# Last output weights read twice in small pieces, operands of the cosine layers moved in time

## The chip, the cores and the metric

One core of a Trainium2 chip runs the whole program in one launch. The time is that of the device, in microseconds, from runs of the same program on the same kind of chip; the kernel before has a median of 1354.78 us in three runs (1353.57 to 1355.01).

## What is computed

Three parts follow each other. Attention with a window of 128 and 4 sink positions gives 1536 rows of 512. Eight experts, weighted by a matrix that is normalised by rows and columns in turn, work on these rows; then two dense layers with a cosine between them.

```python
x = attention(q, k, v)                       # 1536 x 512
P = sinkhorn(exp(x @ w_gate - max))          # 1536 x 8, eight rounds
out = sum over e of P[:, e:e+1] * (relu(x @ w1[e]) @ w2[e])      # w1[e]: 512 x 1024, w2[e]: 1024 x 512
h = out @ w_in                               # 512 x 2048
result = (h * cos(h)) @ w_out                # 2048 x 512
```

## The kernel before

**Layers, batches, stages.** The 1536 rows are two batches of 768. Ten layers run one after the other: e = 0 to 7 are the experts, e = 8 and 9 the two halves of the dense block, each with 1024 of the 2048 hidden columns. Each layer runs on batch 0 and then on batch 1. One layer on one batch is called a stage here and written (e, b), so the cosine stages are (8,0), (8,1), (9,0) and (9,1), in this order.

**A stage.** The first product uses a scheme with seven products in place of eight. Every 32-bit operand is split into a 16-bit high half and a low half, and a product takes three matmuls per pair (high by high, high by low, low by high). In a cosine stage `g1_sums` makes, for each of four column groups j, the seven products in the order o = 0, 4, 1, 5, 2, 3, 6; each is six matmuls into one of five PSUM banks (`ring["g1"]`). The product o = 0 is copied out by ScalarE (L1007), the others are taken up by VectorE adds (L999). `act_cos` then makes h cos(h) for each of four sums per j: ScalarE L893, VectorE L896, ScalarE L901 and L902, VectorE L905, and GpSimd L907 and L909, which write the two halves of `hh`. The second product (`g2_mm`, L1036) takes `hh` and `W2S[e % 2]`, the split w2; part of it is done between the products of `g1_sums` from j = 1 on, in the order f = 0, 4, 1, 5, 2, 6, 3, 7 of the eight pieces of hidden columns.

**Ticks.** The order of all work outside these loops is written by hand. `tick()` is called after each product of the first kind and after each two f of the second: 28 ticks (`GT`) in the first part of a stage, 24 (`HT_`) in the second, 104 in a layer. `put(t0, every, steps)` puts steps at a tick, counted from the call. A tick only says where in each engine's queue an instruction stands; an engine goes through its queue as fast as its operands allow. `late` holds what is put into the queues one tick after.

**Splitting.** `split` (L190, L191) has ScalarE write the high half (a scaled copy) and, one tick later, VectorE the low half from the source and the high half. The scale comes from `scales`: a row maximum, some short VectorE operations, one small TensorE product with a diagonal matrix (L142, L149) to bring the maximum over the partitions together, and four short VectorE operations.

**Weights of layer e + 1** are made ready while layer e runs. `w_load` reads the tensor in four pieces of 512 KB into the one buffer `st`; a maximum of each piece follows, then the scale, then the split. For the first product (`w1_split`) GpSimd makes four sums `S` for each j (L274 to L277) into one of the two buffers with the tag `f64`, and ScalarE and VectorE split them into `W1O`; there is only one `W1O`, so this runs while the second part of (e, 1) runs. For w2 of layer 9 the maximum of a piece is a maximum of squares on ScalarE (L171, `junk` takes the unused output). Its reads stand at tick 0 of layer 8, the squares at ticks 6, 11, 16 and 21, the scale at 26, the eight splits from tick 41 on, every 1.4 ticks. The reads of w1 follow into the same `st` at tick 51, the maxima at 57 to 66, its split at ticks 90 to 97. `w2_first` is used for layer 0 alone: it reads w2 in four pieces into `f64` buffers, once for the maxima and once more for the split.

**Operands of layer 8.** `x2(b)` is called once the experts are summed in `ACC`. For each batch it makes six operands by `x_operand`: three sums on GpSimd (L205 to L207), three splits into a tile `xs` with the tag `f64`, and, after four ticks, a DMA that transposes `xs` into `XO[b]` (L213, issued by SP). All products of a stage read all six. Batch 0's six stand at ticks 5, 12, 19, 26, 33 and 40 of (7,1), batch 1's at ticks 5, 12, 19, 37, 41 and 45 of (8,0). SP's queue also issues the weight reads (L242 in `w_load`, L1123 in `w2_first`) and the output writes.

Of the kernel before, what the change touches and what calls it, by code (L numbers as in the profile page):

```python
# [12 lines left out]
BF16 = mybir.dt.bfloat16  # L13
# [27 lines left out]
def kernel(  # L41
# [14 lines left out]
    nc = tc.nc  # L56
# [746 lines left out]
    def experts(before):  # L803
# [60 lines left out]
        def x2(b):  # L864

            a = ACC[b]
            m = sm.tile([128, NT], F32, tag="x2m", name="x2m")

            def scl():
                m1 = sm.tile([128, 1], F32, tag="x2n", name="x2n")  # L870
                nc.vector.tensor_reduce(out=m1, in_=m, axis=AX.X, op=ALU.max)
                scales(m1, 1, 1e-30, res, f"x2{b}", lambda *s: sx2.__setitem__(b, s))

            def ops(c, i):
                put(2, 1, [x_operand(b, c, i, sx2[b][0])])
# [166 lines left out]
        def layers(e, b, act, so):  # L1042
# [24 lines left out]
            if e == E - 1:  # L1067
                amx, xops = x2(b)

                put(5, 4, [amx[t] for t in tiles])  # L1070
                put(26, 1, amx[-1:])
                if b:

                    put(HT_ + 5, 7.0, xops[:3])
                    put(HT_ + GT + 9, 4.0, xops[3:])
                else:
                    put(HT_ + 5, 7.0, xops)
            late = None
# [35 lines left out]

        def w2_first():

            m = sm.tile([128, NJ], F32, tag="wm", name="wm")
            src = w_src(0, "w2")
            box = {}

            def load(n):
                t = box[n] = stage.tile([128, 2, 512], F32, tag="f64", name="w2p", bufs=2)
                nc.sync.dma_start(out=t, in_=src[:, 2 * (n % NJ):2 * (n % NJ) + 2, :])  # L1123

            def amax(n):
                absmax(m[:, n:n + 1], box.pop(n).rearrange("p a b -> p (a b)"))

            def scl():
                m1 = sm.tile([128, 1], F32, tag="wmm", name="wmm")
                nc.vector.tensor_reduce(out=m1, in_=m, axis=AX.X, op=ALU.max)  # L1130
                scales(m1, 1, 1e-30, res, "w20", lambda *s: wsc.update({(0, "w2"): s}))

            def sp(n):
                f = slice(2 * (n % NJ), 2 * (n % NJ) + 2)
                split(W2S[0][:, 0, f], W2S[0][:, 1, f], box.pop(n), wsc[0, "w2"][0])

            for n in range(2 * NJ):
                put(3.5 * n, 1, [lambda n=n: load(n)])
                put(3.5 * n + 3, 1, [lambda n=n: (amax if n < NJ else sp)(n)])
            put(3.5 * NJ + 3 - 3, 1, [scl])  # L1140

# [21 lines left out]
        for e in range(E + 2):  # L1163
# [98 lines left out]
```

## Time and profile before

| | us |
|---|---|
| median of three runs | 1354.78 |
| lowest, highest | 1353.57, 1355.01 |
| span of the profiled execution, first to last instruction | 1352.8 |
| TensorE busy in it | 1270.7 (94%) |
| VectorE busy | 902.2 (67%) |
| ScalarE busy | 693.1 (51%) |
| GpSimd busy | 645.0 (48%) |

The profiled execution's own time is its span; the runs are measured from outside and lie about 2 us above it. PE is TensorE, DVE VectorE, ACT ScalarE, POOL GpSimd and SP the engine that issues most DMAs. In a row of a timeline stand the start, the duration, the engine, the line, the operation, the tiles written and read, the shapes and, in brackets, how long the engine was idle before and what ended that. TensorE is busy nearly all the time, so what can be read from the trace is where the rest of it lies.

### The profile page before, as it was taken

How to read it: one execution, taken by the hardware profiler on the slowest of the kernel's cores; microseconds unless marked ns; L12 is line 12 of the kernel's file. 1: busy time of each engine (PE TensorE's matmuls, PEld its weight loads, DVE VectorE, ACT ScalarE, POOL GpSimd, SP SyncE). 2: the span in 40 equal slices, each digit the busy share in tenths (PEclk: the TensorE clock that was granted, in tenths of full speed). 3: DMA queues.
4: the chain of work that ended last, by engine and by line, in shares of the span. 5: the costliest groups of instructions: out<-in, count | busy, mean ns of one | idle time of the engine just before them, and what ended most of it. 6: DMA issues, size and time to landing. Idle time of an engine off the chain costs nothing.

```text
span 1352.8 us, 19796 instructions
## 1 busy us (share of the span) xinstructions
PE 1270.7 (94%) x7299; PEld 678.1 (50%) x7299; DVE 902.2 (67%) x1852; ACT 693.1 (51%) x1382; POOL 645.0 (48%) x782
## 2 busy tenths in 40 slices
PE   5657799999999999999999999999999998999998
PEld 3533455454545545455554545555454544445554
DVE  8997952765557753954765485476557688787674
ACT  6555754463636355263534616344471757666452
POOL 4555563521525363263436416333640857377543
PEclk8767999999999999999999999999999999999999
DMA  9899653011112410601231050133102231400001
GB/s 250 160 153 193 155 118 104 1 63 63 63 63 60 143 40 24 194 9 63 79 125 63 16 187 1 63 83 120 63 17 94 55 101 31 103 1 0 32 17 47
DMA packets 140689, 108.78 MB, mean 80 GB/s; under 512 B 100144, under 2 KB 115504, under 8 KB 140592
## 3 DMA queue, kind: packets, MB, share of 16 engines
q1 hardware_dynamic: 126512, 77.22, 22.5%
q0 software_dynamic: 7168, 25.17, 6.1%
q10 hardware_dynamic: 6912, 5.13, 1.5%
q8 instruction: 57, 0.93, 0.3%
q14 instruction: 40, 0.33, 0.1%
HBM read 71.84 MB, written 11.53 MB: 62 GB/s over the span
## 4 chain that ended last, share of the span: by engine, by line
PE 69%; DVE 6%; POOL 4%; issue 3%; ACT 3%; DMA 1%; POOLq 0%; DVEq 0%; ACTq 0%
PE bank L1036 36%; PE bank L968 28%; PE bank L985 4%; DVE tmp L999 2%; DMA xo<-xs 1%; POOL hh L885 1%; DVE tmp L905 1%; DVE tmp L896 1%; DVE w1o L191 1%; ACT xs L190 1%; DVE xs L191 0%; ACT tmp L901 0%; ACT tmp L893 0%; POOL S L276 0%; POOL S L277 0%
## 5 line engine op out<-in xcount | busy, mean ns | idle before, releaser
L1036 PE MATMUL bank<-w2s,hh 128*128 128x512 f16 x2880 | 637.2, 379 | 5.1 <-POOL hh L909 2.7
L968 PE MATMUL bank<-xo,w1o 128*128 128x384 f16 x2688 | 450.6, 328 | 9.7 <-ACT tmp L936 5.2
L1036 PEld LDWEIGHTS <-hh 128*128 128x128 f16 x2880 | 279.9, 98 | 339.7 <-POOL hh L909 5.9
L885 POOL TENSOR_TENSOR hh<-tmp,hh 128x384 f16<-128x384 f32 x256 | 233.4, 931 | 363.3 <-ACT tmp L884 361.5
L968 PEld LDWEIGHTS <-w1o 128*128 128x128 f16 x2688 | 260.7, 98 | 186.4 <-issue 15.0
L936 ACT ACTIVATE tmp<-bank 128x384 f32<-128x384 f32 x192 | 93.3, 487 | 335.7 <-PE bank L968 335.6
L940 DVE TENSOR_TENSOR tmp<-bank,tmp 128x384 f32<-128x384 f32 x192 | 104.1, 553 | 172.1 <-ACT tmp L936 126.3
L985 PE MATMUL bank<-xo,w1o 128*128 128x384 f16 x672 | 120.0, 329 | 6.7 <-ACT tmp L1007 3.6
L1105 DVE SCALAR_TENSOR_TENSOR acc<-bank,PS,acc 128x512 f32<-128x512 f32 x84 | 62.9, 748 | 81.5 <-PE bank L1036 80.9
L883 ACT ACTIVATE hh<-tmp 128x384 f16<-128x384 f32 x192 | 98.9, 515 | 10.4 <-DVE tmp L940 10.4
L884 ACT ACTIVATE tmp<-tmp 128x384 f32<-128x384 f32 x192 | 100.4, 523 | 6.1
L985 PEld LDWEIGHTS <-w1o 128*128 128x128 f16 x672 | 65.9, 98 | 58.4 <-issue 11.0
L907 POOL TENSOR_SCALAR hh<-tmp 128x384 f16<-128x384 f32 x64 | 45.8, 715 | 84.3 <-DVE tmp L905 83.8
L190 ACT ACTIVATE w1o<-S,s 128x1024 f16<-128x1024 f32 x40 | 45.8, 1145 | 74.8 <-POOL S L277 74.2
L168 DVE TENSOR_REDUCE wm<-st 128x1 f32<-128x1024 f32 x68 | 81.5, 1208 | 0.0
L191 DVE SCALAR_TENSOR_TENSOR w1o<-st,s,w1o 128x512 f16<-128x512 f32 x72 | 65.4, 941 | 13.7 <-ACT w1o L190 13.7
L909 POOL TENSOR_TENSOR hh<-tmp,hh 128x384 f16<-128x384 f32 x64 | 68.8, 1075 | 5.3
L191 DVE SCALAR_TENSOR_TENSOR w1o<-S,s,w1o 128x1024 f16<-128x1024 f32 x40 | 54.9, 1373 | 20.9 <-ACT w1o L190 20.9
L999 DVE TENSOR_TENSOR tmp<-bank,tmp 128x384 f32<-128x384 f32 x112 | 59.1, 547 | 10.4 <-PE bank L985 6.3
L191 DVE SCALAR_TENSOR_TENSOR w2s<-st,s,w2s 128x512 f16<-128x512 f32 x72 | 56.5, 798 | 9.7 <-ACT w2s L190 9.5
L190 ACT ACTIVATE w2s<-st,s 128x512 f16<-128x512 f32 x72 | 46.6, 708 | 22.8 <-DVE s L160 22.8
L580 POOL TENSOR_TENSOR parts<-xo,parts 128x512 f16<-128x512 f32 (+1 forms) x38 | 42.0, 1107 | 33.7 <-ACT parts L575 28.6
(187 smaller groups left out, 1320.2 us busy)
## 6 DMA issues: line engine op xcount, KB each, us to landing
st<-in_moe_w_dram SPq DMA_DIRECT2D x56, 512.0 KB, 6.2
f<-in_moe_w_in_dram POOLq DMA_DIRECT2D x16, 512.0 KB, 4.5
f<-in_moe_w_out_dram POOLq DMA_DIRECT2D x16, 512.0 KB, 4.3
w2p<-in_moe_w_dram SPq DMA_DIRECT2D x8, 512.0 KB, 4.4
w_in<-x POOLq DMA_DIRECT2D x16, 256.0 KB, 4.6
w_out<-x POOLq DMA_DIRECT2D x16, 256.0 KB, 4.3
st<-w_out SPq DMA_DIRECT2D x8, 512.0 KB, 5.6
st<-w_in SPq DMA_DIRECT2D x8, 512.0 KB, 6.8
```

The source lines that it names most:

```text
L168: nc.vector.tensor_reduce(out=dst, in_=src, axis=axis, op=ALU.max, apply_absolute_value=True)
L190: nc.scalar.activation(out=hi, in_=src, func=AF.Copy, scale=s)
L191: late.append(lambda: nc.vector.scalar_tensor_tensor(out=lo, in0=src, scalar=s, in1=hi, op0=ALU.mult, op1=ALU.subtract))
L883: nc.scalar.activation(out=hi, in_=src, func=AF.Relu)
L884: nc.scalar.activation(out=dst, in_=src, func=AF.Relu)
L885: nc.gpsimd.tensor_tensor(out=lo, in0=dst, in1=hi, op=ALU.subtract)
L936: nc.scalar.activation(out=t, in_=ps, func=AF.Copy)
L940: nc.vector.tensor_tensor(out=t, in0=ps, in1=t, op=ALU.add)
L968: nc.tensor.matmul(ps, W1O[:, j0 + c, wi, o, kk, :], XO[b][:, kk, o, xi, :], start=(n == 0 and o in (0, 5, 1)), stop=(n == 5), skip_group_ ...
L985: nc.tensor.matmul(ps, W1O[:, j, wi, o, kk, :], XO[b][:, kk, o, xi, :], start=(n == 0), stop=(n == 5))
L999: nc.vector.tensor_tensor(out=t, in0=x, in1=y, op=ALU.add)
L1036: nc.tensor.matmul(ps, HH[:, hi, f, t * 128:(t + 1) * 128], w[:, wi, f, :], start=(f == order[0] and n == 0), stop=(f == order[-1] and n = ...
```

## The change

Four things change. Batch 0's six operands of layer 8 stand every 5 ticks instead of every 7, from the same first tick, and their three sums are made by VectorE instead of GpSimd. Batch 1's six stand every 6 ticks, without the pause in the middle. `w2_first` becomes `w2_pieces`, with the ticks as arguments, and `w2_first` calls it with what it had. And w2 of layer 9 is no longer read into `st`: `w2_last` has it read in four pieces into `f64` buffers at ticks 42, 43, 47 and 48 of layer 8, squared on ScalarE at 46, 47, 51 and 52, its scale at tick 55, which is tick 3 of (8,1), and read again at ticks 99, 99, 104 and 106, in the order of pieces 0, 2, 1, 3, to be split at ticks 103, 105, 109 and 111; layer 9 begins at tick 104. Each split is of a whole piece, 128 x 1024, four in place of eight of 128 x 512. The ticks of w1 of layer 9 stay.

```diff
             def ops(c, i):
-                put(2, 1, [x_operand(b, c, i, sx2[b][0])])
+                put(2, 1, [x_operand(b, c, i, sx2[b][0], g=nc.gpsimd if b else nc.vector)])
...
                 if b:
-                    put(HT_ + 5, 7.0, xops[:3])
-                    put(HT_ + GT + 9, 4.0, xops[3:])
+                    put(HT_ + 5, 6.0, xops)
                 else:
-                    put(HT_ + 5, 7.0, xops)
+                    put(HT_ + 5, 5.0, xops)
...
-        def w2_first():
+        def w2_pieces(e, top, loads, tops, scale, order, reloads, splits):
...
             def load(n):
                 t = box[n] = stage.tile([128, 2, 512], F32, tag="f64", name="w2p", bufs=2)
-                nc.sync.dma_start(out=t, in_=src[:, 2 * (n % NJ):2 * (n % NJ) + 2, :])
+                nc.sync.dma_start(out=t, in_=w_src(e, "w2")[:, 2 * n:2 * n + 2, :])
...
-            for n in range(2 * NJ):
-                put(3.5 * n, 1, [lambda n=n: load(n)])
-                put(3.5 * n + 3, 1, [lambda n=n: (amax if n < NJ else sp)(n)])
-            put(3.5 * NJ + 3 - 3, 1, [scl])
+            for n in range(NJ):
+                put(loads[n], 1, [lambda n=n: load(n)])
+                put(tops[n], 1, [lambda n=n: amax(n)])
+            put(scale, 1, [scl])
+            for k, n in enumerate(order):
+                put(reloads[k], 1, [lambda n=n: load(n)])
+                put(splits[k], 1, [lambda n=n: sp(n)])
...
+        def w2_last():
+            junk = W2S[1][:, 0, 0:2].rearrange("p f w -> p (f w)").bitcast(BF16)
+            w2_pieces(
+                E + 1, lambda d, x: squares(d, x, junk), (42, 43, 47, 48), (46, 47, 51, 52), 55,
+                (0, 2, 1, 3), (99, 99, 104, 106), (103, 105, 109, 111))
...
                 if e == E:
-                    t2, t1 = (0, 6, 5.0, 41, 1.4), (GT + HT_ + -1, GT + HT_ + 5, 3.0, GT + HT_ + GT + 10, 0.5)
+                    t1 = (GT + HT_ + -1, GT + HT_ + 5, 3.0, GT + HT_ + GT + 10, 0.5)
+                    w2_last()
...
-                put(t2[0], 0, ld2[:4])
-                put(t2[1], t2[2], ld2[4:])
-                put(t2[3], t2[4], w2_split(e + 1, st))
+                if e != E:
+                    put(t2[0], 0, ld2[:4])
+                    put(t2[1], t2[2], ld2[4:])
+                    put(t2[3], t2[4], w2_split(e + 1, st))
```

## Rows read from the trace of the kernel before

**Rows 1.** Windows, (7,0) to (9,0): length, busy (count) by engine, clock, DMA share, GB/s.

```profile
980.63:1039.07 58.44, 58.44 (x315) 30.53 (x313) 36.86 (x64) 24.90 (x52) 18.48 (x23) 1.00 0.20 64
1039.07:1098.52 59.45, 58.81 (x315) 30.57 (x314) 39.88 (x64) 36.68 (x74) 40.19 (x48) 1.00 0.22 42
1098.52:1167.90 69.38, 61.37 (x315) 30.60 (x314) 56.37 (x116) 49.43 (x92) 39.76 (x50) 0.98 0.33 72
1167.90:1230.71 62.81, 59.28 (x315) 30.21 (x313) 49.34 (x86) 37.47 (x67) 41.00 (x47) 1.00 0.13 38
1230.71:1290.22 59.51, 58.72 (x314) 30.39 (x313) 42.11 (x74) 30.79 (x57) 31.17 (x34) 1.00 0.06 23
```

**Rows 2.** Timeline of VectorE: first L999 and last L905 of the cosine stages.

```profile
1102.35 0.56 DVE L999 TENSOR_TENSOR tmp<-bank,tmp 128x384 f32<-128x384 f32 x1
...
1150.48 0.73 DVE L905 SCALAR_TENSOR_TENSOR tmp<-tmp 128x384 f32<-128x384 f32 x1 [0.46 <-ACT tmp L902]
...
1171.56 0.56 DVE L999 TENSOR_TENSOR tmp<-bank,tmp 128x384 f32<-128x384 f32 x1 [3.07 <-PE bank L985]
...
1213.28 0.73 DVE L905 SCALAR_TENSOR_TENSOR tmp<-tmp 128x384 f32<-128x384 f32 x1 [0.46 <-ACT tmp L902]
...
1236.46 1.48 DVE L999 TENSOR_TENSOR tmp<-bank,tmp 128x384 f32<-128x384 f32 x3
...
1272.56 0.72 DVE L905 SCALAR_TENSOR_TENSOR tmp<-tmp 128x384 f32<-128x384 f32 x1 [0.46 <-ACT tmp L902]
...
1292.44 0.56 DVE L999 TENSOR_TENSOR tmp<-bank,tmp 128x384 f32<-128x384 f32 x1 [0.66 <-PE bank L985]
```

**Rows 3.** Timeline of TensorE in (8,0) and (8,1): three waits.

```profile
1100.62 4.55 PE L985 MATMUL bank<-xo,w1o 128*128 128x384 f16 x27 [1.45 <-DMA xo<-xs]
...
1138.90 3.51 PE L985 MATMUL bank<-xo,w1o 128*128 128x384 f16 x12 [3.20 <-ACT tmp L1007]
...
1169.83 10.40 PE L985 MATMUL bank<-xo,w1o 128*128 128x384 f16 x63 [1.27 <-DMA xo<-xs]
```

**Rows 4.** In (8,0): VectorE's waits (us, times, longest); timelines of ScalarE and VectorE.

```profile
DVE xs L191 <- ACT xs L190: 7.1, 6, 2.4
...
1135.66 1.04 ACT L171 ACTIVATE w2s<-st 128x1024 bf16<-128x1024 f32 x1
...
1142.70 0.14 DVE L254 TENSOR_REDUCE wmm<-wm 128x1 f32<-128x4 f32 x1
...
1143.82 0.79 DVE L142 TENSOR_SCALAR diag<-eye,p 128x128 bf16<-128x128 bf16 x1
...
1147.45 0.28 DVE L154 TENSOR_REDUCE allm<-bank 128x1 f32<-128x128 f32 x1
```

**Rows 5.** VectorE by line and shape, whole span: the dearest sum of an operand.

```profile
L206 DVE TENSOR_TENSOR hh<-acc,hh 128x128 f32<-128x128 f32 x3 | 2.5, 849 | 0.1
```

**Rows 6.** w2 in small pieces, in layer 0: split by engine (us, mean ns), reads.

```profile
L190 ACT ACTIVATE w2s<-w2p,s 128x1024 f16<-128x1024 f32 x4 | 4.6, 1140 | 0.0
...
L191 DVE SCALAR_TENSOR_TENSOR w2s<-w2p,s,w2s 128x1024 f16<-128x1024 f32 x4 | 5.2, 1289 | 1.8 <-ACT w2s L190 1.6
...
DMA to landing us min/median/max: 3.9/4.4/9.0
```

**Rows 7.** Around (9,0)'s start: timelines of GpSimd, VectorE, ScalarE; VectorE's waits until 1273.4.

```profile
1232.26 1.17 POOL L277 TENSOR_TENSOR S<-st,S 128x256 f32<-128x256 f32 x1
...
1230.17 1.54 DVE L191 SCALAR_TENSOR_TENSOR w1o<-S,s,w1o 128x1024 f16<-128x1024 f32 x1 [0.93 <-ACT w1o L190]
...
1234.64 1.28 DVE L191 SCALAR_TENSOR_TENSOR w1o<-S,s,w1o 128x1024 f16<-128x1024 f32 x1 [0.94 <-ACT w1o L190]
...
1235.65 0.49 ACT L1007 ACTIVATE tmp<-bank 128x384 f32<-128x384 f32 x1
...
DVE tmp L905 <- ACT tmp L902: 1.4, 5, 0.5
DVE tmp L999 <- ACT tmp L1007: 1.4, 3, 0.5
```

More of the change, by code (lines that the diff above doesn't have):

```diff
@@ L1113, in g2_out @@
                 nc.sync.dma_start(out=out[g * 128:(g + 1) * 128, :], in_=o)
-        def w2_first():
+        def w2_pieces(e, top, loads, tops, scale, order, reloads, splits):
             m = sm.tile([128, NJ], F32, tag="wm", name="wm")
-            src = w_src(0, "w2")
             box = {}
@@ L1122, in load @@
                 t = box[n] = stage.tile([128, 2, 512], F32, tag="f64", name="w2p", bufs=2)
-                nc.sync.dma_start(out=t, in_=src[:, 2 * (n % NJ):2 * (n % NJ) + 2, :])
+                nc.sync.dma_start(out=t, in_=w_src(e, "w2")[:, 2 * n:2 * n + 2, :])
             def amax(n):
-                absmax(m[:, n:n + 1], box.pop(n).rearrange("p a b -> p (a b)"))
+                top(m[:, n:n + 1], box.pop(n).rearrange("p a b -> p (a b)"))
             def scl():
@@ L1130, in scl, with w2_first @@
                 nc.vector.tensor_reduce(out=m1, in_=m, axis=AX.X, op=ALU.max)
-                scales(m1, 1, 1e-30, res, "w20", lambda *s: wsc.update({(0, "w2"): s}))
+                scales(m1, 1, 1e-30, res, f"w2{e}", lambda *s: wsc.update({(e, "w2"): s}), top is not absmax)
             def sp(n):
-                f = slice(2 * (n % NJ), 2 * (n % NJ) + 2)
-                split(W2S[0][:, 0, f], W2S[0][:, 1, f], box.pop(n), wsc[0, "w2"][0])
-            for n in range(2 * NJ):
-                put(3.5 * n, 1, [lambda n=n: load(n)])
-                put(3.5 * n + 3, 1, [lambda n=n: (amax if n < NJ else sp)(n)])
-            put(3.5 * NJ + 3 - 3, 1, [scl])
+                f = slice(2 * n, 2 * n + 2)
+                w = W2S[e % 2]
+                split(w[:, 0, f], w[:, 1, f], box.pop(n), wsc[e, "w2"][0])
+            for n in range(NJ):
[5 more added lines that the diff above has]
+                put(splits[k], 1, [lambda n=n: sp(n)])
+        def w2_first():
+            t = [3.5 * n for n in range(2 * NJ)]
+            u = [x + 3 for x in t]
+            w2_pieces(0, absmax, t[:NJ], u[:NJ], 3.5 * NJ, range(NJ), t[NJ:], u[NJ:])
+        def w2_last():
[3 more added lines that the diff above has]
+                (0, 2, 1, 3), (99, 99, 104, 106), (103, 105, 109, 111))
         banks(A0=(2,), A1=(7,), B0=(3,), B1=(3,), C=(6,), g2=(5, 7), l=(5,))
@@ L1170, in experts @@
             if e + 1 < E + 2:
-                junk = W2S[1][:, 0, 0:2].rearrange("p f w -> p (f w)").bitcast(BF16) if e == E else None
-                ld2, ld1 = w_load(e + 1, "w2", None, st, junk), w_load(e + 1, "w1", None, st)
+                ld2, ld1 = w_load(e + 1, "w2", None, st), w_load(e + 1, "w1", None, st)
                 t2, t1 = (3, 9, 3.0, 28, 2.25), (GT + HT_ + -16, GT + HT_ + 6, 2.5, GT + HT_ + GT + 0, 1.0)
```

## Prediction

> **What bounds the kernel now.** I cut the last part of the trace at the first TensorE product of each stage and asked for the windows between the cuts [rows 1]. A stage is one layer and one batch: (7,0) is the last expert on batch 0, (8,0) and (8,1) the first half of the cosine block, (9,0) and (9,1) the second half; (9,0) is the third cosine stage. (7,0) takes 58.44 us with TensorE busy all of it, so this is the floor. Above it lie 1.0 us in (7,1), 10.9 in (8,0), 4.4 in (8,1) and 1.1 in (9,0). What a change here can win is in these 17.4 us, most of it in (8,0).
>
> Next I asked when VectorE's part of a cosine stage ends, the last L905 [rows 2]. Counted from the stage's start that is 52.7 us in (8,0) (1151.21 - 1098.52), 46.1 in (8,1) and 42.6 in (9,0). Against the losses 10.9, 4.4 and 1.1 this is a rule of the kernel: **a cosine stage loses what VectorE's end is later than about 41.7 us**. TensorE's waits show the same from the other side [rows 3]: it stands for the transposed operand at the start of (8,0) and (8,1), and for 3.20 us at 1138.90 for a bank that a late copy still holds. The twelve matmuls behind that gap took 3.51 us; at the pace of the first row (27 in 4.55) they take 2.0, and the granted clock of the stage is 0.98 [rows 1]. So I price every edit by what it does to VectorE's end in its stage.
>
> From its first L999 to its last L905 VectorE takes 36.8 us in (9,0), which holds nothing but the cosine work, and 48.9 in (8,0) [rows 2]. The 12.0 us between them are the scale chain of w2, 2.5 (1.9 from 1142.70 to 1144.61, and four operations after the product from 1147.45, 0.28 and three as short as the first: 0.6) [rows 4], a like and shorter chain for the second batch's scale, which I put at 1.4, and 8.1 for three operands, 2.7 each. Most of that is waiting: VectorE stood 7.1 us, six times, for ScalarE's half of an operand's split [rows 4].
>
> **The change, part by part.** The sum is made on the profiled execution (span 1352.8 us); the median of the runs, 1354.8, is 2.0 us above that span, and I add the difference to the median.
>
> (7,1): the first batch's operands come every 5 ticks, and their three sums go from GpSimd to VectorE. Three sums cost VectorE at most 3 x 0.85 us by the dearest row of them, in attention [rows 5], so six sets 15 us, in a stage where it is busy 40 of 59 [rows 1]. Work that fits costs nothing, but one operand more now falls among the products. Bounds: -1.0 (all that the stage loses) to +2.5 (half a microsecond for each of five operands). I take +0.3, nearest to the stage itself, which lost 1.0 with four operands among its products.
>
> (8,0), start: the six transposes are ten ticks earlier, so TensorE's 1.45 us for them go [rows 3], and VectorE, late from the same backlog, makes its first add about 2.2 us after the start, as in (9,1), where it made it at 3.83 [rows 2]: -1.6. The w2 scale chain leaves: -2.5. Four squares of 1.04 us leave ScalarE's queue [rows 4]; three of them stand shortly ahead of a split that VectorE waits for, so -3.1, between 0 and -4.2. Against that, the second batch's operands now come at ticks 5, 11, 17, 23, 29 and 35, where three of six came after tick 28, in a part where VectorE has room. The fourth falls wholly into the critical part and the fifth by half: 1.5 x 2.7 = +4.0 (bare work without waits, (8.1 - 7.1)/3 = 0.3 each: +0.5; two whole ones: +5.4). The eight splits of w2 that leave the end of (8,0) free nothing that was late. Sum -3.2, bounds -7.8 to +1.3.
>
> (8,1): TensorE's wait for the transposes goes [rows 3]; the last square now stands before ScalarE's first copy, so VectorE's first add comes some 2.5 us after the start, not 3.66 [rows 2]: -1.1. The w2 scale chain arrives at its tick 3: +2.5. Sum +1.4, bounds +0.3 (half the chain fits into waits) to +2.5 (nothing won at the start).
>
> (9,0), and here is the price. The reads at ticks 99 to 106 go into the two f64 buffers, which the four S tiles of w1's split used just before. GpSimd finishes the last S at 1233.43, 2.7 us after (9,0) has begun at 1230.71, and VectorE lets the two buffers go at 1231.71 and 1235.92, 1.0 and 5.2 us after [rows 7]. This lag is carried along: S starts when GpSimd has finished hh, which follows VectorE's end, as the stage's end does. SP holds the reads until the buffers are free; behind them queue only other reads. Such a read lands in 4.4 us [rows 6], so pieces 0 and 2 are there at 5.4 and 9.6. ScalarE has the split of piece 0 in front of its first copy, which so ends at 7.0 at the soonest (5.4 + 1.14 + 0.49) where it was 5.4 [rows 7], and piece 2 right behind that copy: it stands until 9.6, takes 1.14, and VectorE's half 1.29 [rows 6]: 12.1. VectorE's second add stands behind that half, at 12.1 where it was at 6.2 [rows 2]: +5.9. TensorE has five banks, so it stops at the sixth product for ScalarE's copy and again at the eighth. Pieces 1 and 3 add two halves: +2.7, rounded up for a short wait. VectorE's end moves 8.6 us, and the stage had no room left, as it lost 1.1. Bounds: +2.4, if the four halves, 5.2 us, run without waits and fill the 2.8 us that VectorE stands in this stage [rows 7]; +11.1, with another wait for piece 3 of 1.0 and 1.5 for a clock lowered by the stall, as behind the gap in (8,0). I take +8.6, since the rows of the buffers are of this very place.
>
> The Trainium skill ("DMA: Bandwidth & Descriptors", section "Anatomy of one DMA - SWDGE (gpsimd) path") fits one DMA, on another issuing path, as about 2.0 us plus its bytes at 436 GB/s, an estimate of 3.2 us for 512 KB. By it piece 2 would land 1.2 us earlier and the whole sum be 1.2 less. The rows of such reads have 3.9 us as the shortest [rows 6], so they decide.
>
> (9,1) has none of this and stays. Sum: 0.3 - 3.2 + 1.4 + 8.6 = **+7.1 us**; 1354.8 + 7.1 = **1361.9 us**.
>
> **The rivals.** *The work fills idle time (faster).* VectorE's 7.1 us of waits in (8,0) are room: with the squares gone the operands cost their bare work, and in (9,0) the halves fall into the idle 2.8 us because the pieces have landed. Then -1.0 - 7.8 + 0.3 + 2.4 = -6.1: 1348.7. It decides as long as VectorE's end in (9,0) stays below about 45 us. For it: ScalarE is busy only 31 of 59 us in (9,0) [rows 1]. Against it: the times at which the buffers come free. *The reads do not wait, but the work counts (no change).* If S comes early enough, the halves cost 5.2 in (9,0), and with the best of (8,0): 0.3 - 7.8 + 1.4 + 5.2 = -0.9: 1353.9. For it: nothing queues ahead of the reads on SP. Against it: S follows VectorE's end. *Too many operands (slower still).* The upper bounds of (7,1) and (8,0): 2.5 + 1.3 + 1.4 + 8.6 = +13.8: 1368.6. For it: six waits with three operands. *That the operands come no sooner* would leave 1.6 and 1.1 us unwon and is inside the range.
>
> **How the numbers follow.** Forecast 0.55, faster 0.14, no change 0.16, slower still 0.15. A measurement of this kernel can tell 0.2%, 2.7 us. So faster 0.14, same 0.16, slower 0.70. The range leaves out most of the faster rival and the upper part of the last one: 1352 to 1368.
>
> **What would show it.** The windows: (8,0) near 66 us instead of 69.4, (8,1) near 64, (9,0) near 68 instead of 59.5. No wait for the transposes at the start of (8,0) and (8,1). In (9,0) a TensorE gap at the sixth and a longer one at the eighth product; ScalarE standing for w2p reads; those reads issued only when VectorE's last w1o halves are done. It is wrong if the pieces have landed before ScalarE comes to them, if the last L905 of (9,0) comes before 45 us, or if (8,0) falls below 63 us.

## The result and the profile after

The changed kernel takes 1370.26 us (median of four runs, 1369.82 to 1373.22) against 1354.89 for the kernel before: ratio 1.0118, 95% interval 1.0106 to 1.0130. It is slower by some 15.4 us. The prediction had the sign right and the size wrong: +7.1 us and a range that ended at 1368.

The profiled execution has a span of 1368.1 us, 15.3 more than before. The windows from (7,0) to (9,0), cut as in [rows 1]; the columns are start:end, length, busy (count) of PE, PEld, DVE, ACT and POOL, the granted clock, the DMA share and GB/s:

```profile
979.41:1037.85 58.44, 58.44 (x315) 30.55 (x314) 36.85 (x64) 24.90 (x52) 16.86 (x20) 1.00 0.19 64
1037.85:1097.81 59.96, 58.81 (x316) 30.59 (x315) 48.99 (x84) 36.62 (x74) 33.29 (x35) 1.00 0.24 47
1097.81:1173.97 76.16, 65.24 (x314) 31.04 (x313) 49.73 (x98) 43.57 (x82) 38.26 (x47) 0.91 0.32 77
1173.97:1236.78 62.81, 59.51 (x315) 30.28 (x314) 50.37 (x92) 38.40 (x69) 41.00 (x47) 1.00 0.05 20
1236.78:1305.76 68.98, 61.23 (x313) 30.66 (x312) 46.97 (x78) 35.26 (x61) 32.04 (x34) 0.98 0.15 50
```

Against [rows 1] the stages moved by +0.5 in (7,1), **+6.8 in (8,0)**, 0.0 in (8,1) and **+9.5 in (9,0)**; (7,0) and (9,1) have the same length in both. That is 16.8 us. The program came to (7,0) 1.2 us sooner than in the profiled execution of before, which leaves 15.6 of it; the 0.3 to the span's 15.3 were won in and behind (9,1). The forecast was +0.3, -3.2, +1.4 and +8.6, so the miss is 10.0 us in (8,0); the other three are off by +0.2, -1.4 and +0.9.

VectorE's busy time in (8,0) fell from 56.37 to 49.73 us, as was expected of a stage that loses the splits and the scale chain of w2. Its end, which the prediction used as its measure, moved a little too: the last L905 ends 51.96 us after the stage's start (1147.73 + 2.04 - 1097.81), where it was 52.69 [rows 2]. And still the stage is 6.8 us longer. In the kernel before, TensorE's last 79 matmuls of the stage ran through without a stop:

```profile
1150.84 17.22 PE L1036 MATMUL bank<-w2s,hh 128*128 128x512 f16 x79 [0.36 <-POOL hh L909]
```

The timelines of the changed kernel, VectorE's last L905 and then TensorE, ScalarE and GpSimd behind that point (start, duration, engine, line, operation, count, idle before and its releaser), show why:

```profile
1147.73 2.04 DVE L905 SCALAR_TENSOR_TENSOR tmp<-tmp 128x384 f32<-128x384 f32 x2
...
1143.99 1.04 PE L1036 MATMUL bank<-w2s,hh 128*128 128x512 f16 x2 [2.36 <-POOL hh L907]
1145.39 6.22 PE L1036 MATMUL bank<-w2s,hh 128*128 128x512 f16 x16 [0.36 <-POOL hh L909]
1156.21 17.92 PE L1036 MATMUL bank<-w2s,hh 128*128 128x512 f16 x72 [4.60 <-ACT acc L1107]
1173.97 6.01 PE L985 MATMUL bank<-xo,w1o 128*128 128x384 f16 x36
...
1154.86 0.72 ACT L190 ACTIVATE xs<-T,s 128x512 f16<-128x512 f32 x1 [5.47 <-POOL T L207]
1155.49 1.82 ACT L1107 ACTIVATE acc<-bank,scl 128x512 f32<-128x512 f32 x3
...
1152.18 0.91 POOL L909 TENSOR_TENSOR hh<-tmp,hh 128x384 f16<-128x384 f32 x1
1153.05 0.72 POOL L205 TENSOR_TENSOR T<-acc 128x256 f32<-128x256 f32 x1
...
1154.38 0.45 POOL L207 TENSOR_TENSOR T<-acc,T 128x128 f32<-128x128 f32 x1
```

ScalarE evicts the banks of the second product (L1107, which is L1108 in the listing of before). At 1155.49 it evicts three of them in one go, because it had stood for 5.47 us ahead of them. It stood at the split of the sums of the sixth operand, an instruction that comes before the evictions in its queue. Those sums were GpSimd's, and GpSimd made them only at 1153.05, right behind its last hh. TensorE was out of banks and stood for 4.60 us, from 1151.6 on.

In (8,1) the length stays the same, 62.81 us, though the wait for the transposes went and the chain came, and at the start of (8,0) and (8,1) TensorE no longer waits for transposes. In (9,0) the timelines of SP, ScalarE, VectorE and TensorE show the forecast picture:

```profile
1237.81 10.60 SPq L1121 DMA_DIRECT2D w2p<-w_out  x4
...
1241.44 1.15 ACT L190 ACTIVATE w2s<-w2p,s 128x1024 f16<-128x1024 f32 x1 [0.19 <-DMA w2p<-w_out]
...
1245.55 1.15 ACT L190 ACTIVATE w2s<-w2p,s 128x1024 f16<-128x1024 f32 x1 [2.01 <-DMA w2p<-w_out]
...
1246.73 1.28 DVE L191 SCALAR_TENSOR_TENSOR w2s<-w2p,s,w2s 128x1024 f16<-128x1024 f32 x1 [2.36 <-ACT w2s L190]
1247.93 1.01 DVE L999 TENSOR_TENSOR tmp<-bank,tmp 128x384 f32<-128x384 f32 x2
...
1288.33 0.72 DVE L905 SCALAR_TENSOR_TENSOR tmp<-tmp 128x384 f32<-128x384 f32 x1 [0.46 <-ACT tmp L902]
...
1236.78 5.04 PE L985 MATMUL bank<-xo,w1o 128*128 128x384 f16 x30
1243.59 2.11 PE L985 MATMUL bank<-xo,w1o 128*128 128x384 f16 x12 [1.77 <-ACT tmp L1007]
1248.54 5.74 PE L985 MATMUL bank<-xo,w1o 128*128 128x384 f16 x24 [2.84 <-DVE tmp L999]
```

The first read goes out 1.0 us after the stage's start (1237.81 - 1236.78) and the second, of piece 2, 5.2 us after it (1242.02), both as forecast. TensorE makes five products (30 matmuls), stops before the sixth for ScalarE's copy, makes two and stops before the eighth. VectorE's part ends 52.3 us after the start (1288.33 + 0.72 - 1236.78).

### The profile page after: what moved, and what is told of

The parts are those of the page before. It is cut to its first block, busy times and chain, and to the rows that moved or that the text cites. A ratio compares the mean times of both kernels' runs of the same rounds, so it can differ in the third digit from the quotient of the medians.

```text
span 1368.1 us, 19807 instructions
## 1 busy us (share of the span) xinstructions
PE 1277.8 (93%) x7299; PEld 679.9 (50%) x7299; DVE 909.4 (66%) x1866; ACT 692.2 (51%) x1378; POOL 635.7 (46%) x764
## 4 chain that ended last, share of the span: by engine, by line
PE 71%; DVE 6%; ACT 4%; POOL 3%; issue 2%; DMA 1%; POOLq 0%; DVEq 0%; ACTq 0%
PE bank L1036 39%; PE bank L968 28%; PE bank L985 3%; DVE tmp L999 2%; DVE tmp L905 1%; POOL hh L909 1%; DVE tmp L896 1%; ACT tmp L901 1%; POOL hh L907 1%; ACT w2s L190 1%; DVE xs L191 0%; ACT tmp L893 0%; ACT tmp L902 0%; POOL S L276 0%; ACT xs L190 0%
## 5 line engine op out<-in xcount | busy, mean ns | idle before, releaser
L968 PEld LDWEIGHTS <-w1o 128*128 128x128 f16 x2688 | 261.0, 98 | 186.4 <-issue 15.4
L999 DVE TENSOR_TENSOR tmp<-bank,tmp 128x384 f32<-128x384 f32 x112 | 59.2, 547 | 26.8 <-ACT tmp L1007 23.9
L191 DVE SCALAR_TENSOR_TENSOR w1o<-st,s,w1o 128x512 f16<-128x512 f32 x72 | 65.9, 948 | 15.3 <-ACT w1o L190 15.3
L564 ACT ACTIVATE xo<-xo,nm 128x260 f32<-128x260 f32 (+1 forms) x96 | 41.8, 483 | 32.6 <-DVE nm L550 28.1
L191 DVE SCALAR_TENSOR_TENSOR w2s<-st,s,w2s 128x512 f16<-128x512 f32 x64 | 50.4, 796 | 9.6 <-ACT w2s L190 9.5
```

Of the source, the lines that this page charges most:

```text
L191: late.append(lambda: nc.vector.scalar_tensor_tensor(out=lo, in0=src, scalar=s, in1=hi, op0=ALU.mult, op1=ALU.subtract))
L968: nc.tensor.matmul(ps, W1O[:, j0 + c, wi, o, kk, :], XO[b][:, kk, o, xi, :], start=(n == 0 and o in (0, 5, 1)), stop=(n == 5), skip_group_ ...
L999: nc.vector.tensor_tensor(out=t, in0=x, in1=y, op=ALU.add)
```

## The experiments

Two theories stood for (8,0). One is the **place in the queue**: the sixth operand's split stands ahead of the evictions and blocks them until its sums are there. The other is the **load**: six operands are too much work for the stage, on GpSimd or VectorE, wherever they stand. For (9,0) the question was how much of the 9.5 us is waiting for the reads and how much the work itself. Each kernel differs from the one named in brackets, and a cut in an edit is marked by three dots. The ratios are to the kernel before, run alongside (its medians there are 1354.12 to 1356.05). As the part ahead of (7,0), which no edit touches, took 978.5 to 983.7 us in the profiled executions, the stages are compared and not only the medians.

**The sixth operand behind the evictions** (the changed kernel, one operand moved):

```diff
-                    put(HT_ + 5, 6.0, xops)
+                    put(HT_ + 5, 6.0, xops[:5])
+                    put(HT_ + 38, 1.0, xops[5:])
```

> The changed kernel with one edit: the second batch's sixth operand stands at tick 38 of (8,0), not 35, so that ScalarE's split of its sums comes behind the evictions of the first three tiles of the second product, not ahead of them. Theory 'queue' (that split waits 5.47 us for GpSimd's sums and holds three evictions, for which TensorE stood 4.60 us and then ran 2 us at the lower clock): the gap goes, (8,0) falls from 76.2 to 69 to 70 us, the time by 6 to 7. Theory 'amount' (VectorE and GpSimd have too much to do in (8,0), the gap is only where it shows): a gap comes back elsewhere, (8,0) stays above 75, the time within 1.5 of the changed kernel.

Measured: 1368.14 us, ratio 1.0102 (1.0087 to 1.0117). The stages: (8,0) **69.23** in place of 76.16, (8,1) 64.45 in place of 62.81, (9,0) 69.04. VectorE's end in (8,0) stays at 51.97. The window of (8,0), TensorE's timeline behind the first wait for hh, and ScalarE's:

```profile
1100.81:1170.04 69.23, 62.90 (x315) 30.52 (x314) 49.27 (x98) 42.65 (x80) 38.29 (x47) 0.95 0.28 64
...
1147.01 1.03 PE L1036 MATMUL bank<-w2s,hh 128*128 128x512 f16 x2 [2.36 <-POOL hh L907]
1148.41 21.79 PE L1036 MATMUL bank<-w2s,hh 128*128 128x512 f16 x88 [0.36 <-POOL hh L909]
...
1154.35 1.25 ACT L1108 ACTIVATE acc<-bank,scl 128x512 f32<-128x512 f32 x2
1157.89 0.72 ACT L190 ACTIVATE xs<-T,s 128x512 f16<-128x512 f32 x1 [2.29 <-POOL T L207]
```

The same work on the same engines, one split moved by three ticks, and (8,0) is 6.9 us shorter. The sums come no sooner: the split of the sixth operand begins 57.1 us after the stage's start in both (1157.89 - 1100.81, and 1154.86 - 1097.81) and still waits for GpSimd, but the evictions now stand ahead of it. The 88 matmuls that took 6.22 + 17.92 us with a gap of 4.60 between them now run through in 21.79: 4.60 of the 6.9 was the gap, and 2.35 is pace. That is lost to the granted clock. The windows of the changed kernel over these matmuls (the third column from the end is the clock):

```profile
1141.60:1145.40 3.80, 1.08 (x4) 0.15 (x4) 3.56 (x7) 2.42 (x6) 3.06 (x5) 0.77 0.63 121
1145.40:1151.60 6.20, 6.20 (x16) 1.95 (x17) 6.18 (x8) 3.92 (x9) 5.88 (x8) 0.59 0.00 0
1151.60:1156.20 4.60, 0.01 (x1) 0.00 (x0) 1.21 (x3) 1.34 (x3) 2.99 (x5) 0.75 0.53 100
1156.20:1160.00 3.80, 3.79 (x9) 1.28 (x9) 0.75 (x6) 1.11 (x2) 0.00 (x0) 0.50 0.70 131
1160.00:1164.00 4.00, 4.00 (x18) 1.76 (x17) 0.00 (x0) 0.19 (x1) 0.00 (x0) 0.91 0.72 249
```

And the two of the kernel of this run that answer to the second and the third of these:

```profile
1148.40:1154.60 6.20, 6.19 (x17) 2.04 (x18) 5.69 (x8) 4.79 (x11) 5.88 (x8) 0.58 0.00 0
1154.60:1159.20 4.60, 4.60 (x23) 2.06 (x21) 1.21 (x3) 1.72 (x3) 3.02 (x5) 1.00 0.52 100
```

Both lose the same in the first window (the wait of 2.36 us for hh, from 1141.6 in the one and 1144.6 in the other, stands ahead of it in both). Then the one works on and is at full clock, and the other stands, and has the lower level (0.50 of 2.4 GHz) for the 3.8 us after the gap. So the place in the queue is shown; the load is refuted as the cause of these 6.9 us. Two other runs below, which leave (8,0) as it is in the changed kernel, have 76.37 and 76.57 us there.

The median fell by 2.1 us only, where 6 to 7 were expected. In the profiled executions 1.6 us are lost again in (8,1), and the part ahead of (7,0) took 3.0 us more (982.42 where it was 979.41). The +1.6 in (8,1) is a second effect of the same move. The reads of w2 into the `f64` buffers go out as long after the stage's start as before (60.5 us in both), but the stage is by then almost over, and ScalarE stands for them with its squares, four times:

```profile
ACT w2s L171 <- DMA w2p<-w_out: 7.6, 4, 4.8
```

These are 7.6 us in all. In the changed kernel it never stood for them. The first copy of (8,1) comes behind the last square, 3.8 us after that stage's start, where it was 1.8.

**The second batch's sums on VectorE too** (the changed kernel):

```diff
-                put(2, 1, [x_operand(b, c, i, sx2[b][0], g=nc.gpsimd if b else nc.vector)])
+                put(2, 1, [x_operand(b, c, i, sx2[b][0], g=nc.vector)])
```

> The changed kernel with one edit: the second batch's sums are made by VectorE too, as the first batch's are, at the same ticks. It takes 18 sums (1.6 to 2.2 us an operand) from GpSimd in (8,0) and gives VectorE about 1 us for each of six. 'Queue': ScalarE no longer waits 5.47 us for GpSimd, the 4.60 us gap goes, but four to five operands put 4 to 5 us more before VectorE's last L905: (8,0) 73 to 75 us, VectorE's end 55 after the start. 'Amount': the same work lies on the fuller engine: (8,0) 78 us or more and the gap is still there.

Measured: 1372.31 us, ratio 1.0129 (1.0113 to 1.0144); (8,0) 77.02, VectorE's end 55.02. TensorE and ScalarE in (8,0):

```profile
1157.17 17.32 PE L1036 MATMUL bank<-w2s,hh 128*128 128x512 f16 x72 [4.19 <-ACT acc L1107]
...
1155.82 0.72 ACT L190 ACTIVATE xs<-T,s 128x512 f16<-128x512 f32 x1 [3.49 <-DVE T L207]
```

GpSimd is free of the sums (28.3 us busy in place of 38.3) and the gap stays: now the split waits for VectorE's sums, which stand behind VectorE's own work of the stage's end. Whichever engine makes them, they are late there, and the split ahead of the evictions waits. The theory of the queue had forecast that the gap would go, and this was missed. Taking the sums off GpSimd does not take the gap away; but as VectorE's load grew by them, this run alone does not part the two theories. The run with the sixth operand moved does.

**The first batch alone** (the kernel before, only with the first batch's operands every 5 ticks and their sums on VectorE):

```diff
-                put(2, 1, [x_operand(b, c, i, sx2[b][0])])
+                put(2, 1, [x_operand(b, c, i, sx2[b][0], g=nc.gpsimd if b else nc.vector)])
...
-                    put(HT_ + 5, 7.0, xops)
+                    put(HT_ + 5, 5.0, xops)
```

> The kernel before with one part of the change: the first batch's operands every 5 ticks and their sums on VectorE. By the prediction: no wait for the transposes at the start of (8,0), VectorE's first add 1.6 us earlier, (8,0) 67.8 instead of 69.4, (7,1) 0.3 to 0.5 longer, the time 1 to 1.5 us less. Rival: the start was hidden, (8,0) stays at 69 to 69.5, and the time is the same or up to 0.5 more for the sums in (7,1).

Measured: 1352.91 us in ten runs, ratio **0.9987** (0.9978 to 0.9997). (7,1) and (8,0):

```profile
1036.93:1096.89 59.96, 58.81 (x316) 30.61 (x314) 48.99 (x84) 36.50 (x74) 33.30 (x35) 1.00 0.31 69
1096.89:1164.66 67.77, 61.49 (x316) 30.78 (x315) 54.59 (x113) 49.42 (x92) 38.33 (x47) 0.97 0.26 49
```

(7,1) +0.5 and (8,0) -1.61, where the prediction had +0.3 and -1.6 for the start. VectorE's first add comes at 2.22 and its end moves from 52.69 to 51.06: the gain at the start arrives at the end undiminished. This part alone beats both kernels.

**Both operand changes, w2 as before** (the kernel of the last run, and the second batch's six every 6 ticks):

```diff
-                    put(HT_ + 5, 7.0, xops[:3])
-                    put(HT_ + GT + 9, 4.0, xops[3:])
+                    put(HT_ + 5, 6.0, xops)
```

> The kernel before with both operand changes (first batch every 5 ticks with sums on VectorE, second batch every 6 ticks), w2 of layer 9 as before. Against the run with the first batch alone ((8,0) 67.8 us) it tells what the second batch's ticks cost in (8,0). Theory 'queue and operands': two operands more before VectorE's last L905 (+4 to +5.4) and the wait of TensorE for three evictions (+4.6, and 2 for the clock): (8,0) 77 to 80 us, (8,1) 62 to 63, (9,0) 59.5; time 7 to 10 above the kernel before. Rival (the long (8,0) comes from w2's pieces, their reads and squares, in its second part): (8,0) 68 to 70, time within 1 of the first batch alone.

Measured: 1365.33 us, ratio 1.0059 (1.0044 to 1.0074); (8,0) 78.91, (8,1) 61.39, (9,0) 59.53. The window of (8,0), TensorE's longest gap in it, and ScalarE's waits for the sums (us, times, longest):

```profile
1102.05:1180.96 78.91, 65.84 (x315) 31.78 (x314) 56.20 (x117) 48.82 (x92) 38.53 (x47) 0.91 0.21 45
...
1162.65 18.47 PE L1036 MATMUL bank<-w2s,hh 128*128 128x512 f16 x72 [5.13 <-ACT acc L1107]
...
ACT xs L190 <- POOL T L207: 7.3, 2, 5.5
```

The second batch's ticks alone make (8,0) 11.1 us longer (78.91 - 67.77), with the same wait in front of the evictions. They move VectorE's end by only 3.1 (51.06 to 54.15). In (8,1) they win 1.4, the wait for the transposes.

**The maximum of w2 made one stage sooner** (the kernel with the first batch alone; the reads, the squares and the scale chain of w2 of layer 9 put into (7,1), in eight small reads into buffers that are free there, so that (8,0) has neither squares nor chain):

```diff
...
+            put(54, 2.0, [lambda f=f: load(f) for f in range(NF)])
+            put(57, 2.0, [lambda f=f: top(f) for f in range(NF)])
+            put(73, 1, [scl])
...
-                put(t2[1], t2[2], ld2[4:])
+                if e != E:
+                    put(t2[1], t2[2], ld2[4:])
+                if e == E - 1:
+                    w2_top()
```

> The kernel before with the first batch's operands as in the change, and w2 of layer 9 otherwise: its maximum of squares is taken in (7,1), from eight reads of one f into the free x buffers (ticks 2 to 16, squares at 5 to 19, scale at 21), so that (8,0) has neither squares nor the scale chain; read into st at tick 0 of (8,0) and split at ticks 41 to 52 as before. If VectorE's end sets a cosine stage, (8,0) loses 2.5 for the chain and 0 to 4.2 for the squares: from 67.8 to 61 to 65 us, (7,1) longer by less than 1, the others as before; time 3 to 6 below the first batch alone. Rival (the squares and the chain ran in idle time): (8,0) stays above 67, time as with the first batch alone or above.

Measured: 1358.68 us in twelve runs, ratio 1.0020 (1.0012 to 1.0028); (7,1) 64.94, (8,0) 65.02.

```profile
1040.55:1105.49 64.94, 60.55 (x316) 31.08 (x315) 49.23 (x95) 41.13 (x90) 33.06 (x35) 0.97 0.37 85
1105.49:1170.51 65.02, 61.29 (x315) 30.67 (x314) 53.33 (x102) 45.31 (x84) 39.23 (x47) 0.97 0.28 53
```

Squares and chain together are worth 2.75 us in (8,0) (67.77 - 65.02; VectorE's end 51.06 to 48.32), not the 2.5 + 3.1 = 5.6 of the prediction. In (7,1), where they were put here, the squares stand between ScalarE's copies: TensorE stands 3.5 us for these, where it stood 1.2 with the first batch alone, the granted clock is 0.97, and the stage is 5.0 us longer. So by the ratios the time is 4.5 us above that of the first batch alone, where 3 to 6 below it were expected.

**The chain alone, put later** (the kernel with the first batch alone, w2's scale chain at tick 33 in place of 26):

```diff
-                put(t2[1], t2[2], ld2[4:])
+                put(t2[1], t2[2], ld2[4:8])
+                put(33 if e == E else t2[1] + 4 * t2[2], 1, ld2[8:])
```

> The kernel before with the first batch's operands as in the change, and the scale chain of w2 of layer 9 at tick 33 of (8,0), behind the cosine work, not at 26; the squares stay at 6 to 21, the splits at 41. Taking squares and chain out of (8,0) together had moved VectorE's end from 51.1 to 48.3 us. If the chain is most of that (as its 2.5 us of work say): VectorE's end 48.4 to 49, (8,0) 65 to 65.7 instead of 67.8, and the squares are worth under 0.5. If the squares are most of it (as the prediction had it, 3.1 us): VectorE's end above 50, (8,0) above 67. Time 2 to 3 below the first batch alone, or the same.

Measured: 1355.68 us in twelve runs, ratio 1.0009 (0.9997 to 1.0022); (8,0) 69.54, (8,1) 61.36.

```profile
1151.17 0.22 PE L149 MATMUL bank<-diag,one 128*128 128x128 bf16 x1 [3.27 <-DVE diag L142]
1151.23 18.29 PE L1036 MATMUL bank<-w2s,hh 128*128 128x512 f16 x84
```

VectorE's end does come 1.2 us sooner (51.06 to 49.88). So much the chain costs there, and by difference the other 1.6 of the 2.75 are the squares. But the stage is 1.8 longer than without the move, which neither theory had: TensorE has a small product in that chain, its place in TensorE's queue moved by the same seven ticks, and now TensorE stood 3.27 us for VectorE's diag. (8,1) is 1.4 shorter, as TensorE no longer waits for the transposes at its start.

**The maxima of w1 later too** (the run of the chain alone; the maxima and the scale of w1 moved in the same way in (8,1), and the last three operands every 2.5 ticks):

```diff
-                    put(HT_ + GT + 9, 4.0, xops[3:])
+                    put(HT_ + GT + 9, 2.5, xops[3:])
...
+                if e == E:
+                    t1 = (t1[0], GT + HT_ + GT + 1, 1.0, *t1[3:])
```

> The kernel before with the first batch's operands as in the change, and three things that no cosine result waits for moved behind the last L905 of their stage: w2's scale chain to tick 33 of (8,0); the maxima and the scale of layer 9's w1 to ticks 81 to 85, 29 to 33 of (8,1), from 57 to 69; the second batch's last three operands every 2.5 ticks (37, 39, 42) instead of every 4, so that the transposes are there when (8,1) starts. If VectorE's end sets the stages: (8,0) 65 to 65.7, VectorE's end in (8,1) 38 to 40 and (8,1) 58.6 to 59.5 instead of 62.8; (9,0) at 59.5 or better, as S comes earlier; time 6 to 8 below the first batch alone, 1345 to 1347. If GpSimd or the transposes set (8,1) instead, it stays at 61 or more.

Measured: 1359.68 us in seven runs, ratio 1.0036 (1.0023 to 1.0049); (8,0) 71.23, (8,1) 65.61, (9,0) 58.38. VectorE's end in (8,1) comes 2.8 us sooner than in the kernel with the first batch alone (46.08 to 43.29) and the stage is 2.8 longer, by a wait of 5.26 us for the diag. (9,0) alone wins 1.1: it is then as short as the floor. The 1345 to 1347 us that were expected are missed by 13, as the expectation followed VectorE's end and not TensorE's place in the chain.

(8,0) is 1.7 us longer here than in the run of the chain alone, with a gap of the same length at the same place (3.28 and 3.27 us). The same 84 matmuls behind it took 19.98 us here, at a granted clock of 0.63 for 3.4 us and 0.88 for the next 4.0, and 18.29 there, at 1.00 throughout.

**The chain later still** (the kernel with the first batch alone; the chain at tick 39, the splits of w2 from tick 43.5 every 1.1, and the late operands closer together):

```diff
-                    put(HT_ + GT + 9, 4.0, xops[3:])
+                    put(HT_ + GT + 9, 2.5, xops[3:])
...
-                    t2, t1 = (0, 6, 5.0, 41, 1.4), (GT + HT_ + -1, GT + HT_ + 5, 3.0, GT + HT_ + GT + 10, 0.5)
+                    t2, t1 = (0, 6, 5.0, 43.5, 1.1), (GT + HT_ + -1, GT + HT_ + 5, 3.0, GT + HT_ + GT + 10, 0.5)
...
-                put(t2[1], t2[2], ld2[4:])
+                put(t2[1], t2[2], ld2[4:8])
+                put(39 if e == E else t2[1] + 4 * t2[2], 1, ld2[8:])
```

> The kernel before with the first batch's operands as in the change, w2's scale chain at tick 39 of (8,0) (at 33 TensorE came to its small product 3.3 us before VectorE had the diagonal), the eight splits at 43 to 51, and the second batch's last three operands at 37, 39 and 42. If the chain at 33 failed only because TensorE's queue reached it first: no wait of TensorE for diag in (8,0) above 0.5 us, VectorE's end 49.9, (8,0) 66 to 67 instead of 67.8; the transposes are there for (8,1): 61.4 instead of 62.8; time 2 to 3 below the first batch alone. If the chain costs wherever it stands: (8,0) 68 or more, time the same as the first batch alone.

Measured: 1352.88 us in eleven runs, ratio **0.9980** (0.9972 to 0.9989).

```profile
1100.11:1166.80 66.69, 61.51 (x315) 30.71 (x314) 52.52 (x110) 48.28 (x91) 38.90 (x47) 0.97 0.23 50
...
1153.79 0.22 PE L149 MATMUL bank<-diag,one 128*128 128x128 bf16 x1
```

Six ticks further the small product finds its diag ready, and the 1.1 us of VectorE's end arrive: (8,0) 66.69 against 67.77. (8,1) was expected at 61.4 and has 63.00, as TensorE still waits for the transposes at its start. Of all kernels here this one and the one with the first batch alone are faster than before; they can't be told apart by their medians.

**Four of the second batch's operands late, two early** (the kernel with the first batch alone):

```diff
-                    put(HT_ + 5, 7.0, xops[:3])
-                    put(HT_ + GT + 9, 4.0, xops[3:])
+                    put(HT_ + 5, 7.0, xops[:2])
+                    put(HT_ + GT + 9, 2.7, xops[2:])
```

> The kernel before with the first batch's operands as in the change, and the opposite of the change for the second batch: only two operands among the products of (8,0) (ticks 5 and 12), four behind them (37, 39, 42, 45). Two operands more there had cost VectorE 3.1 us, the whole 11 us with the evictions. If it is symmetric: VectorE's end 1.5 to 2.7 us earlier, 48.4 to 49.6, (8,0) 65 to 66.5; the transposes still late for (8,1), 62.8. Time 1 to 3 below the first batch alone. Rival (the fourth one behind collides with the eight splits): (8,1) 64 or more and no gain.

Measured: 1355.93 us in twelve runs, ratio 1.0008 (0.9999 to 1.0016); (8,0) 65.63, (8,1) 66.74.

```profile
1140.25 0.22 PE L149 MATMUL bank<-diag,one 128*128 128x128 bf16 x1 [2.26 <-DVE diag L142]
...
1169.05 7.15 PE L985 MATMUL bank<-xo,w1o 128*128 128x384 f16 x34 [3.75 <-DMA xo<-xs]
```

One operand fewer among the products moves VectorE's end by 3.3 us (51.06 to 47.78). The stage wins 2.1 of it, as TensorE stands for the diag, and (8,1) loses 3.95, as its first products stand 3.75 us for the last transpose. So the time is above that of the first batch alone, where 1 to 3 us below it were expected. The pause in the kernel before sits about where the two costs meet.

**Where the price of (9,0) lies.** Two runs take the wait for the reads away, in different ways. In the first, the changed kernel reads w2 the second time in eight pieces of half the size into buffers that are free by then, at ticks 99 to 110:

```diff
...
+                for f, tag, t0, t1 in ((0, "x", 99, 103), (1, "x", 99, 103), (4, "z", 99, 105), (5, "x", 104, 107),
+                                       (2, "x", 104, 109), (3, "z", 106, 109), (6, "x", 108, 111), (7, "x", 110, 112)):
+                    put(t0, 1, [lambda f=f, tag=tag: load1(f, tag)])
+                    put(t1, 1, [lambda f=f: sp1(f)])
...
```

> The changed kernel with one edit: the second read of w2 goes in eight reads of one f each into the buffers x and z, which nobody uses then, instead of four of two f into f64, which the S tiles held; the first three reads can go at once. Eight splits of 512 (VectorE 0.80 each, 6.4 us) in place of four of 1024 (5.2 us). Theory 'buffers' (as predicted: the reads wait for S, ScalarE and VectorE wait for the reads): ScalarE does not stand for the first three pieces, no 2.84 us gap of TensorE at the eighth product, (9,0) falls from 69.0 to 64 to 66 us. Rival 'work' (the halves on VectorE cost by themselves, the waits were hidden): (9,0) stays at 69 or rises by the 1.2 us of added work.

In the second, the reads and buffers stay and the splits come later:

```diff
-                (0, 2, 1, 3), (99, 99, 104, 106), (103, 105, 109, 111))
+                (0, 2, 1, 3), (99, 99, 113, 114), (111, 112, 118, 120))
```

> The changed kernel with one edit: in (9,0) the four splits stand at ticks 111, 112, 118 and 120 (the second pair's reads at 113 and 114) and no longer at 103 to 111, so that every read has landed when ScalarE comes to its split; VectorE's work is the same. 'Buffers' (the wait is what costs): (9,0) 60 to 62 us instead of 69.0. 'Work' (the four halves, 5.2 us, in a stage that has no room on VectorE): 65 to 66 us. As predicted from both: about 3.4 us of the 9.5 are waits, 6 are work.

Measured: 1369.79 us, ratio 1.0118 (1.0096 to 1.0139) and 1370.20 us, ratio 1.0100 (1.0087 to 1.0114). The windows of (9,0), of the kernel with the eight reads:

```profile
1237.10:1303.80 66.70, 60.81 (x313) 30.46 (x312) 47.31 (x82) 35.67 (x66) 32.70 (x34) 0.97 0.12 40
```

and of the one with the late splits, with its waits (us, times, longest):

```profile
1239.89:1306.50 66.61, 59.70 (x313) 30.25 (x312) 46.41 (x78) 34.95 (x62) 33.30 (x34) 1.00 0.15 52
...
DVE w2s L191 <- ACT w2s L190: 4.5, 3, 1.8
PE bank L1036 <- ACT w2s L190: 1.8, 1, 1.8
PE bank L1036 <- DVE w2s L191: 0.9, 1, 0.9
```

66.70 and 66.61 us, VectorE's end 50.00 and 49.91. Both ways win the same 2.3 and 2.4 of the 9.5; 7.1 us stay with no read waited for. So much is shown. That these 7.1 are the price of the work, four halves on VectorE of 1.28 us each (5.1) and VectorE's waits for ScalarE's halves, is argued, and an upper bound: each run has a cost of its own, eight halves of 0.75 us (6.0) in the first, and in the second 2.7 us in which TensorE stands for the late halves. The medians did not follow in these two runs (the changed kernel has 1370.26), though the window is 2.3 shorter; the spread of the runs, 2.4 and 6.2 us, covers that, and more isn't claimed of them.

## Why the prediction was right in sign and wrong in size

The stages, in us, as the profiled executions show them, with VectorE's end in (8,0) and what the rule makes of it (floor 58.44, plus the end less 41.7):

| kernel | (7,1) | (8,0) | (8,1) | (9,0) | VectorE's end in (8,0) | (8,0) by the rule |
|---|---|---|---|---|---|---|
| before | 59.45 | 69.38 | 62.81 | 59.51 | 52.69 | 69.4 |
| changed | 59.96 | 76.16 | 62.81 | 68.98 | 51.96 | 68.7 |
| sixth operand late | 59.96 | 69.23 | 64.45 | 69.04 | 51.97 | 68.7 |
| sums on VectorE | 59.96 | 77.02 | 62.80 | 69.04 | 55.02 | 71.8 |
| first batch alone | 59.96 | 67.77 | 62.79 | 59.50 | 51.06 | 67.8 |
| both operand changes | 59.96 | 78.91 | 61.39 | 59.53 | 54.15 | 70.9 |
| maximum sooner | 64.94 | 65.02 | 62.89 | 59.52 | 48.32 | 65.1 |
| chain at 33 | 59.97 | 69.54 | 61.36 | 59.50 | 49.88 | 66.6 |
| maxima of w1 later too | 59.96 | 71.23 | 65.61 | 58.38 | 49.89 | 66.6 |
| chain at 39 | 59.97 | 66.69 | 63.00 | 59.53 | 49.93 | 66.7 |
| four operands late | 59.97 | 65.63 | 66.74 | 59.51 | 47.78 | 64.5 |

**(8,0): the step that failed.** The prediction said of the second batch's operands that three stand at ticks 5 to 17 as before and priced the other three by how far they fall into the critical part: "The fourth falls wholly into the critical part and the fifth by half". The sixth, at tick 35, was priced at nothing, as those after tick 28 lay "in a part where VectorE has room". VectorE has room there; ScalarE's queue has not. The split of the sixth stands ahead of the first evictions and waits for sums that GpSimd can only make behind its last hh. That wait is 6.9 us (the run with the sixth operand late): 4.6 of gap and 2.3 of lower clock behind it. Of the moved operands the prediction followed VectorE's part alone; ScalarE's half, and who waits behind it, is not in its sum.

The rule from which it was priced, VectorE's end less 41.7, holds in five rows of the table within 0.6 us, and fails in six. In five of these (changed, sums on VectorE, both operand changes, chain at 33 and maxima of w1 later too) TensorE's timeline has a gap of 3.3 to 5.1 us that ends 1.5 to 6.5 us after VectorE's end, on an eviction or on a diag. In the sixth, four operands late, which is off by 1.1, TensorE stands 2.26 us for the diag ahead of VectorE's end and runs through from there, so it was not VectorE's end that set the stage. The rule holds where VectorE's end is what TensorE waits for last; nothing in the trace of before could contradict it, as TensorE ran through from there in each stage of it.

The other terms of (8,0): the start, -1.6, came out as -1.61. Squares and chain were put at -5.6 and are worth -2.75: the chain 1.2, where 2.5 had been read as its duration, and the squares, by difference, 1.6, where 3.1 had been read as three squares ahead of a split. That part of this time lay in waits that VectorE had anyhow is likely and not shown. The operands were put at +4.0; without the wait they cost 4.2 (69.23 less 65.02, the stage that has neither squares nor chain and the old operands). The terms add up: 69.38 - 1.61 - 2.75 + 11.14 = 76.16, as measured. So the miss of 10.0 us is 6.9 of the wait, 2.85 of squares and chain, and 0.2 of the operands.

**(7,1)** +0.5 where +0.3 stood. **(8,1)** 0.0 where +1.4 stood. The wait for the transposes is gone (-1.4: 62.81 to 61.39 with both operand changes), and so, by difference, the square and the chain at its start cost 1.4, where 2.5 was put; VectorE's first add came 2.34 us after the start (about 2.5 was forecast).

**(9,0): right, with the price put under the wrong name.** As forecast stand the first two reads, issued 1.0 and 5.2 us after the start, from the buffers [rows 7]; the stops at the sixth and the eighth product; VectorE's end at 52.3, where 42.6 + 8.6 = 51.2 stood; +9.5 for +8.6. The prediction put 5.9 us on the wait for piece 2 and 2.7 on the two other halves. In the trace VectorE's second add came 11.2 us after the start (1247.93 - 1236.78; 12.1 was forecast), 4.9 later than before, and from there to VectorE's end another 4.8 were added. The runs without the wait for the reads won only 2.3 and 2.4. The splits inside the stage, with the waits between ScalarE and VectorE that come with them, cost up to 7.1 without it. The rival "the reads do not wait, but the work counts" had 5.2 for them. So the size is near the forecast in part by luck: one term was 1.0 too high and the other 2.1 too low, and most of the price was not the wait. VectorE's end does set this stage: the rule makes 69.0, 66.7 and 66.6 of it in the changed kernel and the two runs, and 68.98, 66.70 and 66.61 were measured.

The first piece's split on ScalarE began 3.6 us after the issue (1241.44 - 1237.81), shorter than the 3.9 to 9.0 us of such reads in layer 0 [rows 6]. The Trainium skill ("DMA: Bandwidth & Descriptors", section "Anatomy of one DMA - SWDGE (gpsimd) path") gives about 2.0 us plus the bytes at 436 GB/s, an estimate of 3.2 us for 512 KB, on another issuing path. The measured value lies between the two, and it decides.

**The range.** It ended at the rival of too many operands, +13.8, which had the upper bound of (8,0) at +1.3. With 6.8 measured there, that bound was too low by 5.5. Without the wait of 6.9, (8,0) would have stood at -0.1, inside the bounds, so the one wait left out is what takes the time out of the range. Three sums in the prediction are off by 0.1 to 0.2 us, which moves nothing: by its rows the chain's last four operations come to 0.7, the end of VectorE's half of piece 2 to 12.0, and the lower bound of (8,1) to 0.15.

What stays open: why the part ahead of (7,0) differs by up to 5 us between profiled executions, how much of the medians' differences of 1 to 3 us comes from there, and why a gap of the same 3.3 us lowered the clock in one run and not in another.

## What to carry to other kernels

An operation that is moved takes a place in the queue of every engine that has an instruction of it, and the one to look at is that of the engine that was not busy: ask what stands right behind it there, and who stops when that is late. A moved producer with slack and its consumer have to move together (the split behind the evictions, TensorE's small product behind the diag), or the time won on one engine is lost on the other. A work rule taken from one engine's end is good only as long as nothing behind that end can stop.

## What was not expected of the hardware

ScalarE did nothing for 5.47 us while three banks filled whose evictions stood right behind in its queue. The Trainium skill ("PSUM — Partial Sum Buffer", section "Engine vs sequencer instructions") says that the queues of ScalarE, VectorE and GpSimd are strictly first in, first out; this trace agrees with it, in these 5.47 us.

A gap of TensorE can cost more than its length, but its length alone does not say how much. After the 4.60 us without work in the changed kernel the granted clock was 0.50 for 3.8 us and 0.91 for the next 4.0, and the 88 matmuls around it lost 2.35 us by pace. Behind each of the five gaps of 4.2 to 5.1 us in (8,0) it was 0.50 to 0.57 for about 4 us. Behind a gap of 3.3 us it stayed at 1.00 in the run of the chain alone and fell to 0.63 in the run with the maxima of w1 later too. Behind the wait of 2.36 us with little work around it, at 1141.6, it was 0.59 over 6.2 us, and 0.58, 0.53 and 0.83 behind the same wait in three other runs. What a stage loses behind a gap is therefore known here to a microsecond or two, and not better.
